# Pooled attention and a top-1 mixture of experts on one core: other buffers for the raw weights at the head, half tiles that fetch split weights into four sets of buffers, and a new order of issue

## The chip, the core and the metric

The kernel runs on one NeuronCore of a Trainium2 chip. The metric is the device time of one execution in microseconds. Inputs and outputs lie in the core's device memory (HBM). The engines are TensorE (PE), VectorE (DVE), ScalarE (ACT), GpSimd (POOL) and SyncE (SP, which here only starts transfers).

## What is computed

```python
# attention over pooled keys, B=4, 12288 queries each, C=128
kv_pool = kv.reshape(B, H // 4, 4, W // 4, 4, C).mean(axis=(2, 4))
k = v = kv_pool.reshape(B, -1, C) @ w_sr            # 768 keys per batch
s = (q @ k.transpose(0, 2, 1)) / np.sqrt(C)
a = np.exp(s - s.max(-1, keepdims=True)); a /= a.sum(-1, keepdims=True) + 1e-09
x = (a @ v).reshape(B * N, C)                        # 49152 rows of 128
# top-1 mixture of 8 experts, F=1024
logits = x @ w_gate
expert_idx = np.argmax(logits, axis=1)
out[mask_e] = gate_w[mask_e, None] * (np.maximum(x[mask_e] @ w1[e], 0.0) @ w2[e])
```

Here `gate_w` is the softmax probability of the chosen expert.

## The kernel before

All is float32. A product of two float32 matrices is made from three matmuls (`mm3`, lines 230 to 233): each operand is split into a high part (`high`, a rounding copy on ACT) and a low part (`low`, the source minus the high part, on DVE or POOL), and high times high, high times low and low times high add up in PSUM.

**The stages.** The 49152 rows are 96 stages of 512 rows, 24 to a batch. A stage of attention does the scores of four groups of 128 rows (`scores`), their maxima on DVE (`maxima`), the exponentials on ACT (`exps`), and then turns the probabilities: from stage 6 on DVE turns 32x32 blocks (`turn_p`), sixteen transfers move the blocks (`move_p`, tile pb to tile pt), ACT and POOL split them (`high_p` into tile pth, `low_p` in place in pt), and PE multiplies with the values (`values`). The first six stages turn them on PE instead (`turn_first`). Then `route` multiplies with the gate, picks each row's expert, counts places (`ranks`, `places`: the last part of `places`, called pos in the trace, is on POOL), and `put` scatters the rows with four GpSimd transfers into the buffer xs in HBM, sorted by expert. The row numbers that these need are reduced on DVE (tile dst, line 593). Before each stage's rows are filled POOL clears the tail of tile row (line 486), which waits for scatters under way.

**The experts.** From stage 2's end on, whenever 512 rows of an expert are there, `choose` (a chain of nine small DVE steps) picks an expert, and a tile of 512 rows goes through it: `read` loads the rows (tile xb) and their numbers (tokf), DVE turns them (xt, line 791), ACT and POOL split them (xh, xl), and eight blocks f of `first` (x times w1), `high_h` and `low_h` (tiles hh and hlow) and `second` (h times w2) follow. `copy_y`, `turn_y`, `rows_y` and `put` bring the result back to rows and scatter them into the output with GpSimd transfers (line 860) at the numbers in tile tok. There are 94 such full tiles. What is left at the end goes in half tiles of 256 rows (numbers 94 to 99 always, more only if rows are left); in a half tile the numbers are masked on DVE (lines 806 and 809, tile tok with 3 buffers).

**The weights.** At the head `split` (lines 148 to 173) loads each expert's raw w1 and w2 into tile raw (3 buffers, shared with the loads of keys), splits them on ACT and POOL into one of the two resident sets wts, and stores this set to ws in HBM (2 MB an expert). A full tile fetches its expert's set from ws (line 755) only if another expert than two tiles before was chosen. A half tile instead fetches the raw weights (`fetch_whole`, 1 MB) into pb and pt and splits them on the spot (`cut`, four pieces on ACT, and two each on POOL and DVE).

**The order.** `Plan` is a heap of steps, each with a time in units; 16 units are one stage. The table `AT` holds the offsets. Each engine gets its instructions in the order of these times on PE, ACT and DVE; the queues of POOL and SP follow the same plan through the scheduler. An engine works strictly in its own order: a step that waits holds up all behind it. A half tile comes every 8 units, and its expert is chosen shortly before it is fetched (line 894).

Of the kernel before, what the change touches and what calls it, by code (L numbers as in the profile page):

```python
# [21 lines left out]
P = 128  # L22
G = 4
# [9 lines left out]
    "turn_q": -0.15, "high_q": 3.34, "low_q": 5.01, "maxima": 1.13, "exps": 2.45, ("first_p", 0): 5.48,  # L33
    ("first_p", 1): 4.1, ("first_p", 2): 4.74, ("first_p", 3): 5.1, ("first_p", 4): 5.32,
    ("first_p", 5): 7.4, "first_high": 0.5, "first_low": 1.3, "first_values": 2.69, "turn_p": 2.65,
    "move_p": 17.32, ("high_p", 0): 28.78, ("high_p", 1): 25.01, ("high_p", 2): 29.02, "low_p": 0.45,
    ("values", 0): 37.6, ("values", 1): 38.01, ("values", 2): 39.41, ("values", 3): 39.91,
    ("values", 4): 41.61, ("values", 5): 42.21, "copy_x": 0.6, "turn_x": 1.76, "logits": 0.8, "row": 1.7,
    "gate_exp": 2.27, "gate": 2.29, "ranks": 1.12, "places": 2.13, "put_x": 3.83, "expert": 24.43,
    "fetch": -12.69, "read": -9.0, "weights": -5.6, ("cut", 0, 0): -7.93, ("cut", 1, 0): 3.67,  # L40
    ("cut", 0, 1): 1.14, ("cut", 1, 1): 3.1, "turn_m": -4.57, "high_m": 1.58, "low_m": 2.94, "first": 4.6,
    "high_h": 0.0, "low_h": 1.35, "second": 4.85, "copy_y": 0.52, "pads": 4.0, "split": -14.0, "splits": 11.0, "turn_y": 1.61, "rows_y": 4.66,
# [20 lines left out]
def tile_pooled_attention_top1_moe(ctx: ExitStack, tc, q, kv, w_sr, w_gate, w1, w2, out):  # L63
# [84 lines left out]
    def split(t, e):  # L148

        wt, own = wts[e % 2], {}  # L150

        def load():
            for n in range(2):
                own[n] = kp.tile([P, POOL // 2, POOL * C], F32, name="raw", bufs=3)
            nc.sync.dma_start(out=own[0].rearrange("p r c -> p (r c)"), in_=w1[e])
            nc.sync.dma_start(
                out=own[1].rearrange("p r (f d) -> p (r f) d", d=D),
                in_=w2[e].rearrange("(f p) d -> p f d", p=P),
            )

        def cut(n):
            wf = own[n].rearrange("p r c -> p (r c)")
            high(wt[:, 2 * n], wf)
            low(wt[:, 2 * n + 1], wf, wt[:, 2 * n], nc.gpsimd)
# [56 lines left out]
    def load_turned(name, rows, n):  # L221

        blocks = ap.tile([P, T], F32, name=name)
# [435 lines left out]
    def choose(j):  # L659
# [26 lines left out]
        if final:  # L686
# [7 lines left out]
            thr = rp.tile([P, 1], F32, name="thr" + tag, bufs=4)  # L694
# [3 lines left out]
        num = rp.tile([P, 3], I32, name="num" + tag)  # L698
# [42 lines left out]
    def weights(t, j):  # L741
# [17 lines left out]
        def fetch_whole():  # L759
            for n in range(2):  # L760
                own[n] = ap.tile([P, F], F32, name=("pb", "pt")[n])
            nc.sync.dma_start(out=own[0], in_=w1[bass.ds(own["ex"], 1)].rearrange("o p f -> p (o f)"))
            nc.sync.dma_start(
                out=own[1].rearrange("p (f d) -> p f d", d=D),
                in_=w2[bass.ds(own["ex"], 1)].rearrange("o (f p) d -> p (o f) d", p=P),
            )

        def cut(n, c):
            cs = slice(c * T, (c + 1) * T)
            high(wt[:, 2 * n, cs], own[n][:, cs])  # L770
            low(wt[:, 2 * n + 1, cs], own[n][:, cs], wt[:, 2 * n, cs], nc.vector if c else nc.gpsimd)

        at(t + AT["fetch"], where)
        if j < FULL:
            at(t + AT["weights"], fetch)
            return
        at(t + AT["fetch"], fetch_whole)
        for n in range(2):
            for c in range(F // T):
                at(t + AT["cut", n, c], cut, n, c)  # L780

    def experts(t, j):
        own = {}
        wt = wts[j % 2]
# [12 lines left out]
        def low_m():  # L797
# [3 lines left out]
            tok = own["tok"] = rp.tile([P, G], I32, name="tok", bufs=3)  # L801
            if own["thr"] is None:
                nc.gpsimd.tensor_copy(out=tok[:, gs], in_=own["tokf"][:, gs])
            else:
                old = rp.tile([P, G], F32, name="old")
# [5 lines left out]
        def first(f):  # L811
# [3 lines left out]
            hp = own["hp", f] = take()  # L815
            for k in range(per):
                fs = slice((f * per + k) * P, (f * per + k + 1) * P)
                mm3(hp[:, k * n : (k + 1) * n], wt[:, 0, fs], wt[:, 1, fs], own["xh"], own["xl"], True, True)
# [13 lines left out]
        def second(f):  # L832
            y = own["y"] = ps[:, BANK_Y, :n]
            for k in range(per):
# [3 lines left out]
                    y, wt[:, 2, fs], wt[:, 3, fs], own["hh", f][:, ns], own["hl", f][:, ns],  # L838
# [51 lines left out]

    def tile_j(j, u=None):
        t = 16 * (min(j, FULL) + AHEAD + 3) + 8 * max(j - FULL, 0) + AT["expert"]
# [3 lines left out]
        at(t + AT["read"], read, j)  # L896
        experts(t, j)
# [50 lines left out]
```

## Time and profile before

| what | value |
|---|---|
| median of 3 runs | 2346.57 us (2337.69 to 2347.06) |
| the profiled execution's own time | 2344.68 us |
| its span, first to last instruction | 2343.0 us |
| PE busy | 2179.0 us (93%) |
| POOL busy | 1832.5 us (78%) |
| DVE busy | 1777.1 us (76%) |
| ACT busy | 1494.3 us (64%) |
| mean granted TensorE clock | 0.986 |
| moved by the transfers | 324.59 MB |

A row of the timeline gives start and duration in us, engine, line, operation, what it writes and reads, and in brackets the engine's idle time before it and what ended that. A row of the waits gives in total how long one kind of instruction kept its engine idle for another, how often, and the longest. Lines are those of the kernel before.

### The profile page before, as it was taken

To read this page: it belongs to the slowest core of one execution; us is meant where nothing else is said; L and a number is where in the kernel's file an instruction comes from. 1 tells how busy PE (TensorE), PEld (TensorE's weight loads), DVE (VectorE), ACT (ScalarE), POOL (GpSimd) and SP (SyncE) were. 2 spreads that over 40 slices of the span, in tenths; PEclk is the share of its full clock that TensorE was granted. 3 is DMA by queue.
4 is the path that set the end of the run, shared out by engine and by line. 5 is a ranking of instruction groups with operands and counts; after the bars stand their busy time and mean duration, and the time that the engine had idled before them with its cause. 6 is when DMAs were issued, how large, how long until landed. Compare 5 with 4: busy or idle time off the path is not lost.

```text
span 2343.0 us, 41042 instructions
## 1 busy us (share of the span) xinstructions
PE 2179.0 (93%) x10630; PEld 1788.3 (76%) x10630; DVE 1777.1 (76%) x4368; ACT 1494.3 (64%) x3031; POOL 1832.5 (78%) x1957
## 2 busy tenths in 40 slices
PE   6778999999999999999999999999998999999986
PEld 6667877778777787778877777777786878788765
DVE  2566878987777778987786778998776777877564
ACT  2656666666666676666666666666665666666553
POOL 2656888878887888878887888878887888888863
PEclk9999999999999999999999999999999999999997
DMA  8866556655565556655556556665556555554341
GB/s 237 282 191 148 124 133 157 161 122 116 121 156 145 125 116 157 160 139 117 119 143 159 127 119 147 163 146 123 113 151 143 128 119 119 127 119 112 89 116 53
DMA packets 590357, 324.59 MB, mean 139 GB/s; under 512 B 497048, under 2 KB 515609, under 8 KB 588064
## 3 DMA queue, kind: packets, MB, share of 16 engines
q1 hardware_dynamic: 565408, 268.34, 51.0%
q0 software_dynamic: 24704, 53.53, 6.6%
q8 instruction: 87, 1.43, 0.3%
q14 instruction: 158, 1.29, 0.2%
HBM read 287.84 MB, written 72.88 MB: 154 GB/s over the span
## 4 chain that ended last, share of the span: by engine, by line
POOL 31%; PE 21%; DMA 13%; issue 13%; DVE 9%; SPq 8%; ACT 3%; POOLq 0%; DVEq 0%; ACTq 0%
POOL pt L219 18%; PE ps L231 7%; PE ps L232 6%; DMA xs<-row,dst 6%; PE ps L233 6%; POOL out_dram L860 5%; DMA xb<-xs 5%; POOL xs L595 4%; SPq L382 4%; SPq L226 3%; DVE hlow L826 3%; ACT prob L362 2%; POOL pos L586 1%; PE ps L500 1%; DVE pb L371 1%
## 5 line engine op out<-in xcount | busy, mean ns | idle before, releaser
L822 ACT ACTIVATE hh<-ps 128x512 fp32r<-128x512 f32 x776 | 465.3, 600 | 323.4 <-PE ps L233 309.8
L826 DVE SCALAR_TENSOR_TENSOR hlow<-ps,hh 128x512 fp32r<-128x512 f32 x776 | 529.1, 682 | 179.7 <-ACT hh L822 177.8
L219 POOL TENSOR_TENSOR pt<-pt,pth 128x1024 fp32r<-128x1024 f32 x270 | 640.4, 2413 | 2.8 <-ACT pth L216 1.8
L362 ACT ACTIVATE prob<-ps,nmax 128x768 f32<-128x768 f32 x384 | 346.2, 902 | 265.4 <-DVE nmax L354 265.2
L860 POOL DMA_INDIRECT out_dram<-yo,tok x388 | 384.8, 992 | 130.1 <-issue 79.9
L595 POOL DMA_INDIRECT xs<-row,dst x384 | 380.1, 990 | 116.1 <-issue 89.4
L371 DVE STREAM_TRANSPOSE pb<-prob 128x768 f32<-128x768 f32 x360 | 352.1, 978 | 88.5 <-ACT prob L362 78.6
L231 PE MATMUL ps<-xh,wt 128*128 128x512 f32 (+1 forms) x800 | 340.3, 425 | 75.2 <-DVE hlow L826 64.3
L354 DVE TENSOR_REDUCE nmax<-ps 128x1 f32<-128x768 f32 x384 | 364.7, 950 | 51.2 <-PE ps L233 49.9
L231 PE MATMUL ps<-hh,wt 128*128 128x512 f32 (+1 forms) x800 | 323.2, 404 | 0.0
L216 ACT CAST pth<-pt 128x1024 fp32r<-128x1024 f32 x270 | 273.4, 1047 | 69.6 <-DMA pt<-pb 55.2
L232 PE MATMUL ps<-hlow,wt 128*128 128x512 f32 (+1 forms) x800 | 314.1, 393 | 2.7 <-DVE hlow L826 2.7
L232 PE MATMUL ps<-xl,wt 128*128 128x512 f32 (+1 forms) x800 | 314.1, 393 | 1.5 <-POOL xl L219 1.5
L233 PE MATMUL ps<-xh,wt 128*128 128x512 f32 (+1 forms) x800 | 313.7, 392 | 0.0
L233 PE MATMUL ps<-hh,wt 128*128 128x512 f32 (+1 forms) x800 | 312.1, 390 | 0.0
L231 PE MATMUL ps<-kh,qh 128*128 128x384 f32 x768 | 269.7, 351 | 4.6 <-ACT qh L216 2.3
L232 PE MATMUL ps<-kl,qh 128*128 128x384 f32 x768 | 260.4, 339 | 0.0
L233 PE MATMUL ps<-kh,ql 128*128 128x384 f32 x768 | 259.6, 338 | 0.8 <-POOL ql L219 0.8
L231 PEld LDWEIGHTS ps<-xh,wt 128*128 128x128 f32 x800 | 153.4, 192 | 118.2 <-DVE hlow L826 95.1
L232 PE MATMUL ps<-pt,vh 128*128 128x512 f32 x540 | 213.8, 396 | 3.4 <-POOL pt L219 3.4
L231 PE MATMUL ps<-pth,vh 128*128 128x512 f32 x540 | 214.6, 397 | 0.0
L233 PE MATMUL ps<-pth,vl 128*128 128x512 f32 x540 | 213.8, 396 | 0.0
(133 smaller groups left out, 3824.6 us busy)
## 6 DMA issues: line engine op xcount, KB each, us to landing
wt<-ws SPq DMA_DIRECT2D x94, 2048.0 KB
pt<-pb SPq DMA_DIRECT2D x1440, 96.0 KB
raw<-in_kv_dram SPq DMA_DIRECT2D x96, 256.0 KB
qb<-in_q_dram SPq DMA_DIRECT2D x384, 64.0 KB
xb<-xs SPq DMA_DIRECT2D x376, 64.0 KB
ws<-wt SPq DMA_DIRECT2D x8, 2048.0 KB
raw<-in_moe_w_dram SPq DMA_DIRECT2D x16, 512.0 KB
out_dram<-yo,tok POOLq DMA_INDIRECT x388, 2.3
```

The lines of the kernel that those rows point to most:

```text
L216: nc.scalar.copy(out=dst, in_=src)
L219: eng.tensor_tensor(out=dst, in0=src, in1=h.bitcast(F32), op=ALU.subtract)
L231: nc.tensor.matmul(out=ps, lhsT=wh, rhs=xh, start=start, stop=False)
L232: nc.tensor.matmul(out=ps, lhsT=wh, rhs=xl, start=False, stop=False)
L233: nc.tensor.matmul(out=ps, lhsT=wl, rhs=xh, start=False, stop=stop)
L354: nc.vector.tensor_reduce(out=nmax, in_=own["s", g][:, :, :NH], op=ALU.max, axis=AX.XY, negate=True)
L362: nc.scalar.activation(out=prob.rearrange("p (h k) -> p h k", h=2), in_=own["s", g][:, :, :NH], func=AF.Exp, bias=own["nmax", g], scale=1. ...
L371: nc.vector.transpose(out=own["pb"][:, :, :, g, :].rearrange("p c b t -> p b c t"), in_=own["prob", g].rearrange("p (b c t) -> p b c t", c ...
L595: put = nc.gpsimd.indirect_dma_start(out=xs, out_offset=bass.IndirectOffsetOnAxis(ap=dst[:, g : g + 1].bitcast(U32), axis=0), in_=own["row ...
L822: nc.scalar.activation(out=hh, in_=own["hp", f], func=AF.Relu)
L826: nc.vector.scalar_tensor_tensor(out=hl, in0=own["hp", f], scalar=0.0, in1=own["hh", f].bitcast(F32), op0=ALU.max, op1=ALU.subtract,)
L860: put = nc.gpsimd.indirect_dma_start(out=out, out_offset=bass.IndirectOffsetOnAxis(ap=own["tok"][:, g : g + 1].bitcast(U32), axis=0), in_= ...
```

## The change

1. At the head the raw weights go to tile pth (4 buffers, which belong to the high parts of the probabilities and are first used in stage 6) instead of raw. The splits begin at -8 units instead of -14, at almost the same spacing (10.92 instead of 11); the cuts still come 10 and 11 units after the load, and the store to ws is placed 19 units after it instead of 14.
2. Half tiles fetch split weights from ws (2 MB, in two transfers of 1 MB for w1 and w2), with no condition and no `cut`. Tiles 94 and 95 take them into pb and pt, 96 and 97 into the two resident sets, 98 and 99 into pb and pt again. The fetch is placed 26 units before the tile, or where the tile four before it has ended, if that is later.
3. Half tiles read their rows into buffers of raw and prob instead of xb. The experts of tiles 94 to 99 are chosen right after those of the last full tiles, 4.6 units apart.
4. Buffers: tok, tokf and thr have 8 instead of 3, 3 and 4, num 4 instead of 2.
5. The table of offsets has new numbers. In a stage, `values` come up to 2 units earlier, the experts' rows are turned 2.5 units later (`turn_m`), the relu (`high_h`) comes 1.2 units later, `places` 0.8 earlier.

```diff
-    "turn_q": -0.15, "high_q": 3.34, "low_q": 5.01, "maxima": 1.13, "exps": 2.45, ("first_p", 0): 5.48,
+    "turn_q": 0.06, "high_q": 3.87, "low_q": 5.01, "maxima": 1.13, "exps": 2.45, ("first_p", 0): 6.3,
...
-                own[n] = kp.tile([P, POOL // 2, POOL * C], F32, name="raw", bufs=3)
+                own[n] = ap.tile([P, F], F32, name="pth", bufs=4)
...
-        at(t + 10, cut, 0)
-        at(t + 11, cut, 1)
-        at(t + 14, keep)
+        at(t + AT["split_cut"], cut, 0)
+        at(t + AT["split_cut"] + 1, cut, 1)
+        at(t + AT["split_keep"], keep)
...
-        own["xb"], gets = load_turned("xb", rows, size(j))
-        own["tokf"] = rp.tile([P, G], F32, name="tokf", bufs=3)
+        k = (j - FULL) % 6
+        own["xb"], gets = load_turned(*(("xb", rows, size(j)) if j < FULL else
+                                        ("raw", rows, size(j), kp) if k < 3 else ("prob", rows, size(j))))
+        own["tokf"] = rp.tile([P, G], F32, name="tokf", bufs=8)
...
-        def fetch_whole():
-            for n in range(2):
-                own[n] = ap.tile([P, F], F32, name=("pb", "pt")[n])
...
+        def fetch_end():
+            k = (j - FULL) % 4
+            if k < 2:
+                w1p = ap.tile([P, 2, F], F32, name="pb").bitcast(F32R)
+                w2p = ap.tile([P, 2, F], F32R, name="pt")
+            else:
+                w1p, w2p = wts[j % 2][:, :2], wts[j % 2][:, 2:]
+            own["wt"] = (w1p, w2p)
+            for n, w in enumerate(own["wt"]):
+                nc.sync.dma_start(
+                    out=w.bitcast(F32),
+                    in_=ws[bass.ds(own["ex"], 1)].rearrange("o p n f -> p (o n) f")[:, 2 * n : 2 * n + 2],
+                )
...
+        u = start(j - 4) + (size(j - 4) // 32 - 2) + AT["first"] + AT["second"] + 0.1
+        u = t + AT["fetch_end"] if j < FULL + 2 else max(t + AT["fetch_end"], u)
+        at(t + AT["fetch_end"], where)
+        at(u, fetch_end)
...
-            tok = own["tok"] = rp.tile([P, G], I32, name="tok", bufs=3)
+            tok = own["tok"] = rp.tile([P, G], I32, name="tok", bufs=8)
...
-        if ("tile", j) not in state:
-            select(t + AT["fetch"] - 6 if u is None else u, j)
+        if j < SURE:
+            state["chosen"] = state["chosen"] + 4.6 if u is None else u
+        if j != SURE:
+            select(state["chosen"] if j < SURE else t + AT["fetch_end"] - 6, j)
```

What the new numbers do to POOL's queue in a stage in the middle of the run, before (ql is the low part of the queries, xs the scatter of routed rows, row the clearing and numbering of the next rows, xl the low part of an expert tile's rows, out_dram the scatter of results, pt the low parts of the probabilities, pos the places):

```order
L219 TENSOR_TENSOR ql<-qt,qh 128x512
L803 CAST tok<-tokf 128x4
L595 DMA xs<-row,dst 397312x144 x4
L219 TENSOR_TENSOR xl<-xt,xh 128x512
L486 MEMSET row 128x4x15
L487 TENSOR_SCALAR row<-slot 128x4
L860 DMA out_dram<-yo,tok 49152x128 x4
L219 TENSOR_TENSOR pt<-pt,pth 128x4x256 x3
L586 TENSOR_TENSOR pos<-pos,oh 128x8 x3
```

and now:

```order
L218 TENSOR_TENSOR ql<-qt,qh 128x512
L594 DMA xs<-row,dst 397312x144 x4
L867 DMA out_dram<-yo,tok 49152x128 x4
L218 TENSOR_TENSOR xl<-xt,xh 128x512
L808 CAST tok<-tokf 128x4
L485 MEMSET row 128x4x15
L486 TENSOR_SCALAR row<-slot 128x4
L218 TENSOR_TENSOR pt<-pt,pth 128x4x256 x3
L585 TENSOR_TENSOR pos<-pos,oh 128x8 x3
```

The scatter of results moved ahead of xl and of the clearing of row, directly behind the scatter of routed rows. In the 18 stages that also load keys the clearing of row stands directly behind the scatter of routed rows in both kernels, and the scatter of results moved only ahead of xl.

SP's queue at the head, from the second load of weights on, before:

```order
L155 DMA raw<-in_moe_w_dram 128x1024
L141 DMA xs<-pad 512x1x144
L226 DMA qb<-in_q_dram 32x16x32 x4
L156 DMA raw<-in_moe_w_dram 128x8x128
L167 DMA ws<-wt_109 128x4096
L141 DMA xs<-pad 512x1x144 x6
L155 DMA raw<-in_moe_w_dram 128x1024
L156 DMA raw<-in_moe_w_dram 128x8x128
L226 DMA qb<-in_q_dram 32x16x32 x4
L167 DMA ws<-wt_110 128x4096
```

and now:

```order
L156 DMA pth<-in_moe_w_dram 128x1024
L157 DMA pth<-in_moe_w_dram 128x8x128
L225 DMA qb<-in_q_dram 32x16x32 x4
L141 DMA xs<-pad 512x1x144 x8
L225 DMA qb<-in_q_dram 32x16x32 x4
L166 DMA ws<-wt_109 128x4096
L156 DMA pth<-in_moe_w_dram 128x1024
L157 DMA pth<-in_moe_w_dram 128x8x128
L166 DMA ws<-wt_110 128x4096
L156 DMA pth<-in_moe_w_dram 128x1024
```

The eight fills of the pad rows moved ahead of the first store to ws, and no load of weights stands behind a fill any more.

SP's queue at the end, where the first half tiles are fetched (num holds the row, the expert and the condition of a chosen tile; the register instructions between are left out by name), now:

```order
L750 TENSOR_LOAD num
L771 DMA pb<-ws 128x2048
L771 DMA pt<-ws 128x2048
L225 DMA raw<-xs 32x8x32
L731 DMA tokf<-xs 128x2x1
L225 DMA xb<-xs 32x16x32
L731 DMA tokf<-xs 128x4x1
L757 DMA wt_110<-ws 128x4096
```

where before, tile by tile, stood:

```order
L748 TENSOR_LOAD num
L762 DMA pb<-in_moe_w_dram 128x1024
L763 DMA pt<-in_moe_w_dram 128x8x128
L226 DMA xb<-xs 32x8x32
L729 DMA tokf<-xs 128x2x1
```

The fetch and the rows of tile 94 moved ahead of the rows (xb) of the last full tile, 93.

More of the change, by code (lines that the diff above doesn't have):

```diff
@@ L32 @@
 AT = {
-    "turn_q": -0.15, "high_q": 3.34, "low_q": 5.01, "maxima": 1.13, "exps": 2.45, ("first_p", 0): 5.48,
[L34 to L42, printed above, removed]
+    "turn_q": 0.06, "high_q": 3.87, "low_q": 5.01, "maxima": 1.13, "exps": 2.45, ("first_p", 0): 6.3,
+    ("first_p", 1): 4.35, ("first_p", 2): 4.74, ("first_p", 3): 4.29, ("first_p", 4): 5.32,
+    ("first_p", 5): 7.4, "first_high": 0.5, "first_low": 1.3, "first_values": 2.69, "turn_p": 2.92,
+    "move_p": 17.32, ("high_p", 0): 28.78, ("high_p", 1): 25.01, ("high_p", 2): 29.02, "low_p": 0.53,
+    ("values", 0): 35.64, ("values", 1): 37.68, ("values", 2): 39.08, ("values", 3): 38.39,
+    ("values", 4): 41.28, ("values", 5): 41.88, "copy_x": 0.6, "turn_x": 2.27, "logits": 0.8, "row": 1.7,
+    "gate_exp": 2.27, "gate": 2.29, "ranks": 1.12, "places": 1.32, "put_x": 3.83, "expert": 24.43,
+    "fetch": -12.69, "read": -9.0, "weights": -5.6, "turn_m": -2.09, "high_m": 1.16, "low_m": 2.94, "first": 4.6,
+    "high_h": 1.2, "low_h": 1.35, "second": 4.85, "fetch_end": -26.0, "copy_y": 0.52, "pads": 4.0, "split": -8.0,
+    "splits": 10.92, "split_cut": 10.0, "split_keep": 19.0, "turn_y": 1.61, "rows_y": 4.66,
 }
@@ L219, in low, with load_turned @@
         eng.tensor_tensor(out=dst, in0=src, in1=h.bitcast(F32), op=ALU.subtract)
-    def load_turned(name, rows, n):
-        blocks = ap.tile([P, T], F32, name=name)
+    def load_turned(name, rows, n, pool=ap):
+        blocks = pool.tile([P, T], F32, name=name, bufs=3 if name in ("raw", "prob") else 2)
         bv = blocks[:, :n].rearrange("p (t c) -> p t c", c=SQ)
@@ L757, in fetch @@
             )
-        def fetch_whole():
-            for n in range(2):
-                own[n] = ap.tile([P, F], F32, name=("pb", "pt")[n])
[L762 to L773, printed above, removed]
+        def fetch_end():
[11 more added lines that the diff above has]
+                )
+        state["wt", j] = own
         if j < FULL:
+            own["wt"] = (wt[:, :2], wt[:, 2:])
+            at(t + AT["fetch"], where)
             at(t + AT["weights"], fetch)
             return
[L777 to L780, printed above, removed]
+        u = start(j - 4) + (size(j - 4) // 32 - 2) + AT["first"] + AT["second"] + 0.1
+        u = t + AT["fetch_end"] if j < FULL + 2 else max(t + AT["fetch_end"], u)
+        at(t + AT["fetch_end"], where)
+        at(u, fetch_end)
     def experts(t, j):
         own = {}
-        wt = wts[j % 2]
         n = size(j)
@@ L804, in low_m @@
             else:
-                old = rp.tile([P, G], F32, name="old")
+                old = table("old", G)
                 nc.vector.tensor_scalar(
@@ L837, in second @@
                 mm3(
[L838 removed]
+                    y, wt[:, 0, fs], wt[:, 1, fs], own["hh", f][:, ns], own["hl", f][:, ns],
                     fb == 0, fb == FB - 1,
@@ L889, in tiles, with start @@
             tile_j(i - AHEAD, u)
+    def start(j):
+        return 16 * (min(j, FULL) + AHEAD + 3) + 8 * max(j - FULL, 0) + AT["expert"]
     def tile_j(j, u=None):
-        t = 16 * (min(j, FULL) + AHEAD + 3) + 8 * max(j - FULL, 0) + AT["expert"]
-        if ("tile", j) not in state:
-            select(t + AT["fetch"] - 6 if u is None else u, j)
+        t = start(j)
+        if j < SURE:
+            state["chosen"] = state["chosen"] + 4.6 if u is None else u
+        if j != SURE:
+            select(state["chosen"] if j < SURE else t + AT["fetch_end"] - 6, j)
         weights(t, j)
-        at(t + AT["read"], read, j)
+        at(t + AT["read"] if j < FULL else t + AT["fetch_end"] + 0.1, read, j)
         experts(t, j)
```

16 lines of the change are left out of this document (8 added, 8 removed).

## Prediction

> **What bounds the kernel now.** I read the windows view first, over four pieces of the span that lie around what the change touches: the head with the splits, the 2000 us of full tiles, the last full tile, and the half tiles. A row gives the stretch, its length, then busy time and instructions of PE, PE's weight loads, DVE, ACT and POOL, then granted clock, DMA share and GB/s.
>
> ```profile
> 0.00:200.00 200.00, 144.23 (x807) 124.22 (x808) 101.44 (x258) 100.15 (x209) 95.17 (x119) 0.93 0.80 230
> 200.00:2200.00 2000.00, 1926.88 (x9251) 1571.99 (x9250) 1600.15 (x3872) 1328.95 (x2694) 1657.78 (x1756) 1.00 0.58 134
> 2200.00:2265.00 65.00, 59.31 (x267) 45.92 (x267) 37.42 (x130) 34.02 (x66) 45.12 (x51) 1.00 0.35 82
> 2265.00:2343.00 78.00, 48.61 (x311) 46.18 (x309) 38.04 (x110) 31.17 (x64) 34.44 (x33) 0.80 0.28 75
> ```
>
> PE is the bound wherever it is not idle, and its number of matmuls hardly changes. So the change can save no more than PE's idle time and what a lower clock costs. Idle are 200 - 144.23 = 55.8 us at the head, 2000 - 1926.88 = 73.1 us in the middle, 5.7 us in the third piece and 78 - 48.61 = 29.4 us in the half tiles, where the clock is 0.80 besides. Next came the waits view of the middle, to see what PE's idle time there is put down to (total us, times, longest).
>
> ```profile
> PE ps L231 <- DVE hlow L826: 44.3, 56, 2.5
> PE ps L849 <- DVE hlow L826: 13.4, 70, 0.5
> ```
>
> The first is the first matmul of a `first` block, which waits for the DVE step that frees its PSUM buffer. The timeline says why DVE is late, below.
>
> **The half tiles (parts 2, 3, 4).** First the waits view of DVE from 2264 on and then the timeline of PE and DVE. A timeline row is start, duration, engine, line, operation, and the idle time before it with its releaser.
>
> ```profile
> DVE tok L809 <- DMA out_dram<-yo,tok: 19.5, 4, 6.1
> 2264.85 0.28 PE L231 MATMUL ps<-xh,wt 128*128 128x256 f32 x1
> 2265.75 3.52 DVE L219 TENSOR_TENSOR wt<-pt,wt 128x512 fp32r<-128x512 f32 x1
> 2270.26 0.50 PE L232 MATMUL ps<-hlow,wt 128*128 128x512 f32 x1 [2.69 <-DVE hlow L826]
> 2271.24 0.42 PE L231 MATMUL ps<-xh,wt 128*128 128x256 f32 x1
> 2285.33 0.16 DVE L809 TENSOR_TENSOR tok<-old,tokf 128x2 int32<-128x2 f32 x1 [6.06 <-DMA out_dram<-yo,tok]
> 2287.19 0.58 PE L231 MATMUL ps<-xh,wt 128*128 128x256 f32 x1 [5.87 <-DVE hlow L826]
> 2287.57 0.42 PE L232 MATMUL ps<-xl,wt 128*128 128x256 f32 x1
> 2291.20 0.41 PE L231 MATMUL ps<-hh,wt 128*128 128x256 f32 x1
> 2292.08 0.28 PE L231 MATMUL ps<-xh,wt 128*128 128x256 f32 x1
> 2294.84 0.28 PE L233 MATMUL ps<-hh,wt 128*128 128x256 f32 x1
> 2332.77 0.37 ACT L844 COPY yt<-ps 128x256 f32<-128x256 f32 x1 [1.48 <-PE ps L233]
> ```
>
> Tile tok has 3 buffers. Its fourth user must wait until a scatter of results that reads the old numbers has landed; DVE stands for that four times, 19.5 us, and PE behind it, 5.87 us at 2287. After such a pause the matmuls are slow: from 2287.57 to 2291.20 seventeen of them take 3.63 us, 0.21 each, while the 23 steps from 2292.08 to 2294.84 take 0.12 each. Part 4 gives tok 8 buffers, and six half tiles follow the last full ones, so the wait goes, the pause goes, and with it the slow stretch, about 17 x 0.09 = 1.6 us a time. Part 2 takes all eight pieces of `cut` per half tile off ACT, POOL and DVE. One such piece on DVE, the 3.52 us at 2265.75, made PE wait 2.69 us.
>
> The new time of this piece: six half tiles of 48 matmuls each (eight blocks, two halves of the work, three matmuls) are 288 x 0.12 = 34.6 us. For the turns of the results and the lag of the first and last blocks I estimate 5 us. From the last copy at 2332.77 to the span's end at 2343.0 are 10.2 us, which no edit touches. That makes 50 us against 2343.0 - 2264.85 = 78.2 us now: **-28 us**. I take 1 us off for a late start and say **-27**.
>
> What is late next are the fetches. Six times 2 MB instead of six times 1 MB must come in. In the chain of waits at the head a fetch of the same kind has this row; the second row is the windows view where the present half tiles' weights come in.
>
> ```profile
> 180.13 9.18 DMA wt<-ws
> 2260.00:2270.00 10.00, 7.02 (x34) 5.55 (x34) 9.30 (x24) 5.53 (x12) 7.21 (x7) 1.00 0.71 184
> ```
>
> The first two fetches stand on SP ahead of the last full tile's rows, 26 units before their tiles, some 25 to 30 us, so at about 2240; six of 9.18 us are 55 us, so the last lands around 2295. With the time above the last half tile begins at 2264.85 + 5 x 5.8 = 2294, so the fetch just about does. At 184 GB/s, 2.1 MB take 11.4 us and six 68 us: the last lands at 2308, 14 us late for its first block, of which the wait for w2 lies further on; I price this case at 10 us, so -17. The Trainium skill (*DMA: Bandwidth & Descriptors*, Specifications) gives a core about 358 GB/s from HBM, by which a fetch would be an estimated 5.9 us, all six land before 2280 and never bind; the row of 9.18 us says less, and I go by the row. The last full tile's rows are queued behind such a fetch on SP, at most 9.18 us; the rows are asked for some 9 units, 12 us, ahead of their use, so this costs 0 to 3 us. Ends for the piece: -31 and -17.
>
> On the slow stretch the Trainium skill (*TensorE: Matmul & The Clock Gate*, Part 1) says that the clock halves after at least one idle window of about 3.4 us. The pause of 5.87 us agrees; behind the pause of only 2.69 us at 2270.26 the trace has slow matmuls too (0.42 at 2271.24, against 0.28), which speaks against the bound. By that rule new pauses of 2 to 3 us behind late fetches (R2) would cost no clock, by the row some 1.6 us each on top; with up to six of them that is inside the ends above.
>
> **The middle (part 5).** The timeline of a stage in which PE waits, in order of time:
>
> ```profile
> 711.60 0.15 POOL L486 MEMSET row<- 128x60 f32 x1 [3.22 <-DMA xs<-row,dst]
> 717.30 7.09 POOL L219 TENSOR_TENSOR pt<-pt,pth 128x1024 fp32r<-128x1024 f32 x3
> 724.36 0.75 POOL L586 TENSOR_TENSOR pos<-pos,oh 128x8 f32<-128x8 f32 x3
> 725.47 0.18 DVE L593 TENSOR_REDUCE dst<-pos 128x4 int32<-128x32 f32 x1 [3.80 <-POOL pos L587]
> 725.65 0.68 DVE L826 SCALAR_TENSOR_TENSOR hlow<-ps,hh 128x512 fp32r<-128x512 f32 x1
> 726.39 0.50 PE L231 MATMUL ps<-xh,wt 128*128 128x512 f32 x1 [2.16 <-DVE hlow L826]
> ```
>
> POOL stands 3.22 us at clearing row, since a scatter of routed rows has not landed. So its low parts end late, pos is late, DVE stands 3.80 us at dst, hlow behind it is late, and PE waits 2.16 us. Over the middle the same two waits read:
>
> ```profile
> POOL row L486 <- DMA xs<-row,dst: 92.5, 71, 5.6
> DVE dst L593 <- POOL pos L587: 88.1, 64, 4.2
> ```
>
> The order shows that now, in all but 18 stages, the scatter of results stands between the scatter of routed rows and the clearing of row. Its four pieces last from 1121.01 to 1125.89 in the rows of the next fence, 4.9 us, and with xl behind them POOL has 6 us of work there. 92.5 / 71 = 1.3 us a time, so most of this wait is covered. POOL then reaches its low parts earlier by up to what it waited, and a stage like the one above loses most of its 2.16 us. PE's `values` also stand one block further ahead, so the blocks that wait have about a block more of PE's work in front of them.
>
> How much of the 44.3 us goes? In the 18 stages with keys the clearing keeps its place and its wait stays, which leaves 50 to 53 of 71 stages helped, 0.7 to 0.75. Some of the wait is taken up again by POOL's own work, which is the same amount. I take 60%, **-26 us**. The ends are -44 (all of it) and +10 (the moved xl begins to cost, below). The 13.4 us at the turns of results (L849) are 0.19 us a time for the lag of hlow itself and stay.
>
> The price of the new order is on xl. A stage without that wait, POOL's queue from one pos to the next and PE's use of xl:
>
> ```profile
> 1111.02 0.75 POOL L586 TENSOR_TENSOR pos<-pos,oh 128x8 f32<-128x8 f32 x3
> 1118.54 1.32 POOL L219 TENSOR_TENSOR xl<-xt,xh 128x512 fp32r<-128x512 f32 x1
> 1121.01 1.06 POOL L860 DMA_INDIRECT out_dram<-yo,tok  x1 [0.46 <-ACT xt L430]
> 1123.41 0.40 PE L232 MATMUL ps<-xl,wt 128*128 128x512 f32 x1
> 1125.89 7.15 POOL L219 TENSOR_TENSOR pt<-pt,pth 128x1024 fp32r<-128x1024 f32 x3
> 1132.96 0.80 POOL L586 TENSOR_TENSOR pos<-pos,oh 128x8 f32<-128x8 f32 x3
> ```
>
> xl now ends at 1119.9, 3.5 us before PE reads it. Behind the scatter of results (1125.89 - 1121.01 = 4.9 us) it ends at 1124.8, 1.4 us after 1123.41, if POOL's queue started no earlier. But the places come 0.8 units earlier (16 units are the 21.94 us from 1111.02 to 1132.96, so 1.1 us), and the 0.46 and 0.35 us of small waits here go. So the two are about even: -1.4 + 1.1 + 0.5 = +0.2 us of slack. This is the step on which the forecast is least safe. I cost it at nothing, because a PE that waits here once moves its whole schedule later against POOL's and then has slack, unless POOL's own round is the longer one: 21.94 minus its waits of about 1 us is 20.9, below the period.
>
> Of what else moves, the queries' high parts and the relu (`high_h`) change only their place on ACT, which is idle a third of the middle (2000 - 1328.95), so nothing.
>
> **The head (part 1).** Rows of the timeline:
>
> ```profile
> 46.28 8.96 SPq L141 DMA_DIRECT2D xs<-pad  x6
> 61.37 1.04 ACT L216 CAST wt<-raw 128x1024 fp32r<-128x1024 f32 x1 [7.17 <-DMA raw<-in_moe_w_dram]
> 131.80 4.66 POOL L219 TENSOR_TENSOR wt<-raw,wt 128x1024 fp32r<-128x1024 f32 x2
> 138.46 1.09 PE L402 MATMUL ps<-ident,prob 128*128 128x128 f32 x4 [5.79 <-DVE num L700]
> ```
>
> ACT waited 7.17 us for raw weights queued behind other transfers, and PE behind its exponentials. The splits now begin 6 units later, so ACT does 4 to 6 us of other work first: I take -5. At 138.46 PE waited 5.79 us for a chain that begins with pos, which stood behind 4.66 us of the last split's low parts on POOL; in the new order pos stands ahead of them: -4 of 5.79. Together **-9 us**. The transfers of the head, 0.80 of the DMA engines' time by the first row, are the same in bytes, and the later stores no longer stand ahead of keys; if they now stand ahead of something that PE needs, as the six pads do in SP's queue for 8.96 us, it could cost 5. If all waits of this kind go it is -20. Ends: -20 and +5.
>
> **The sum.** -9 - 26 - 27 = -62 on the profiled execution. Its own time of 2344.68 becomes 2282.7; the median of the runs was 1.9 us above that execution, so **2284**, rounded down from 2284.6.
>
> **The rivals.**
> - R1, the middle gains nothing: POOL's wait goes, but DVE's dst was not what set PE's pace; its next wait is for ACT's hh. For it: the stages are within 3% of PE's busy time. Then -9 - 27 = -36, 2311. Against it: the chain at 711 to 726 is unbroken.
> - R2, the weights bind the half tiles at 184 GB/s: -17 in place of -27 and a middle at half, -13; -39, 2308.
> - R3, slower: PE waits for xl at each tile's first matmul. It decides from 36 / 94 = 0.4 us a tile on, since head and half tiles bring 36. With the 1.4 us of above less 0.5, 0.9 us in the 67 stages with the new order cost 60 us and the middle's gain goes: -36 + 60 = +24, 2371. Against it: the 1.1 us of the earlier places.
> - R4, the change doesn't do what it says in the half tiles: the copy to yo, with 2 buffers, waits for the same scatters as tok did, and DVE or ACT stands again. DVE stood up to 6.1 us for a landing, and half tiles are to be 5.8 us apart, so two buffers are near the edge. -17 for that piece, and 2294.
>
> **How the numbers follow.** Forecast 0.58, R1 0.20, R2 0.08, R3 0.06, R4 0.08. About 0.5%, 11.7 us, is what a measurement of this kernel can tell from no change. The low end of the range is the forecast with 8 of 20 us more of the head, 18 more of the middle and 4 of the half tiles: 2254 if all came at once, I say 2252. The high end takes in R1 with the half tiles at -17 and 0 to 2 us at the head lost: 2322. Outside lie R3 and the far ends, 2 in 10 at most. Faster holds the forecast, R2, R4 and nearly all of R1, and the milder edge of R3 is the same: faster 0.89, same 0.05, slower 0.06.
>
> **What would show it.** Right: in the half tiles no DVE wait at tok, clock near 1.0, and 50 us from the first of their matmuls to the end; in the middle, POOL's wait at row down from 92.5 to some 30 us (the 18 stages with keys), DVE's at dst under 45, PE's at L231 for hlow under 20; at the head no PE wait over 4 us behind POOL's low parts. Wrong: a new PE wait on POOL's xl in the waits view (R3), on a fetch of weights from ws after 2240 (R2), ACT waiting for out_dram at yo (R4), or PE's busy share of the middle still 96% with POOL's wait gone (R1).

## The result, and the profile after

The changed kernel takes **2307.65 us** (median of 4 runs, 2303.95 to 2310.3) against 2345.83 us for the kernel before in the same session: ratio 0.9845, 95% interval 0.9832 to 0.9858. The forecast was 2284 in a range of 2252 to 2322: the sign and the range held, the gain was 38 us where 62 were forecast. By the number alone R2 (2308) and R1 (2311) lie nearer than the forecast; which it was, only the waits can tell. The first four experiments (e1 to e4) ran on another chip than the later ones; there three kernels with the new table took some 300 us more than the same texts took elsewhere, so these three were run again. The gain of the changed kernel came back in its own second series (after_again).

I read the two profiles piece by piece, cut where the same work is done: at the dst step of stage 6, that of stage 92, and the first matmul of a half tile. The columns are those of the windows view. Before:

```profile
0.00:221.59 221.59, 165.65 (x911) 141.94 (x912) 116.70 (x292) 115.14 (x239) 109.69 (x132) 0.94 0.77 219
221.59:2174.66 1953.07, 1882.63 (x9042) 1536.01 (x9041) 1567.00 (x3790) 1299.41 (x2635) 1623.36 (x1721) 1.00 0.58 134
2174.66:2264.85 90.19, 82.01 (x372) 64.03 (x370) 55.16 (x180) 48.41 (x95) 65.00 (x73) 1.00 0.39 93
2264.85:2343.00 78.15, 48.76 (x311) 46.33 (x309) 38.19 (x110) 31.32 (x65) 34.46 (x34) 0.80 0.28 75
```

and the changed kernel:

```profile
0.00:208.04 208.04, 168.46 (x909) 143.77 (x910) 116.50 (x293) 113.86 (x238) 109.60 (x132) 0.92 0.82 232
208.04:2149.99 1941.95, 1871.15 (x9034) 1552.58 (x9033) 1581.09 (x3789) 1311.26 (x2633) 1615.54 (x1721) 0.99 0.58 135
2149.99:2254.65 104.66, 89.03 (x380) 69.75 (x380) 62.14 (x222) 48.54 (x93) 61.78 (x70) 0.93 0.48 126
2254.65:2308.60 53.95, 40.41 (x311) 38.74 (x309) 22.93 (x55) 20.97 (x44) 21.88 (x24) 0.91 0.43 141
```

The head won 13.6 us (forecast 9), the stages 6 to 92 won 11.1, the last full tiles **lost 14.5**, and the half tiles won 24.2 (forecast 27). Together 34.4 us of span (2343.0 to 2308.6). For the last full tiles the forecast had only 0 to 3 us for late rows. Taken with them, what it called the middle, 26 us of gain, came to 11.1 - 14.5, a loss of 3 us.

The two largest of PE's waits from stage 6 to stage 92 in the changed kernel, where the prediction shows those of before:

```profile
PE ps L230 <- DVE hlow L832: 25.1, 4, 6.4
PE ps L231 <- POOL xl L218: 24.4, 19, 2.8
```

The 44.3 us in 56 small waits are gone, and in their place stand four waits of over 6 us and 19 waits for xl. PE's idle time in this piece is as long as before, 70.8 us against 70.4. POOL's wait for the scatter and DVE's wait for pos behaved as forecast or better:

```profile
POOL row L485 <- DMA xs<-row,dst: 35.8, 18, 2.9
DVE dst L592 <- POOL pos L586: 0.9, 1, 0.9
```

92.5 us became 35.8, in just the 18 stages with keys, and 88.1 us became 0.9. So the chain that the prediction read was broken, and the time came back elsewhere. Where, is told by the step from dst to dst. Over 50 of the 60 stages that neither load keys nor change experts a stage took 22.13 us before and 21.42 now: 35 us won. Three stretches with keys (13 to 19, 36 to 43, 60 to 67) took 470.6 us together and now 513.2: 43 us lost. The third of them, rows of DVE in the kernel before and in the changed one:

```profile
1449.05 0.18 DVE L593 TENSOR_REDUCE dst<-pos 128x4 int32<-128x32 f32 x1 [1.21 <-POOL pos L587]
1612.86 0.17 DVE L593 TENSOR_REDUCE dst<-pos 128x4 int32<-128x32 f32 x1
```

```profile
1429.05 0.18 DVE L592 TENSOR_REDUCE dst<-pos 128x4 int32<-128x32 f32 x1
1611.42 0.18 DVE L592 TENSOR_REDUCE dst<-pos 128x4 int32<-128x32 f32 x1
```

163.8 us became 182.4. Inside such a stretch lies this, in order of time in the changed kernel (rows of POOL, DVE and PE):

```profile
893.37 1.32 POOL L218 TENSOR_TENSOR xl<-xt,xh 128x512 fp32r<-128x512 f32 x1
893.81 8.37 DVE L268 TENSOR_TENSOR pooled<-half 128x128 f32<-128x128 f32 x1
895.06 6.96 POOL L218 TENSOR_TENSOR pt<-pt,pth 128x1024 fp32r<-128x1024 f32 x3
902.11 0.68 DVE L832 SCALAR_TENSOR_TENSOR hlow<-ps,hh 128x512 fp32r<-128x512 f32 x1
902.84 0.80 PE L230 MATMUL ps<-xh,wt 128*128 128x512 f32 x1 [6.43 <-DVE hlow L832]
```

The DVE step that adds the two halves of a block of pooled keys (`join`) takes 8.37 us. It begins while POOL runs xl and ends when POOL's low parts end, at 902.0. In the kernel before the same step took a quarter of a microsecond:

```profile
938.44 0.25 DVE L269 TENSOR_TENSOR pooled<-half 128x128 f32<-128x128 f32 x1
938.63 0.97 POOL L860 DMA_INDIRECT out_dram<-yo,tok  x1 [0.31 <-issue]
940.89 7.09 POOL L219 TENSOR_TENSOR pt<-pt,pth 128x1024 fp32r<-128x1024 f32 x3
```

There it fell into the scatter of results, which stood between xl and the low parts; in the changed kernel xl and the low parts follow each other directly. Four of the 18 joins took 7.6 to 9.1 us in the changed kernel, and behind each PE stood for 6.1 to 6.4 us. At the last full tiles PE waits for xl, the longest for 6.25 us:

```profile
2222.95 0.79 PE L231 MATMUL ps<-xl,wt 128*128 128x512 f32 x1 [6.25 <-POOL xl L218]
```

**Theory.** (A) The new numbers win some 50 us in the stages without keys, those where experts change among them. The kernel loses it again by two things that POOL's new order brings: the low parts begin while DVE has its join, a step with two inputs in SBUF that does not get through while POOL computes, and xl stands behind the scatter of results, which makes PE wait in the stages with keys and at the last full tiles. (B) The rival: the stages with keys and the end are bound by DVE's and POOL's amount of work, the long rows are only where that shows, and whatever is taken away, another wait takes its place.

### The profile page after: what moved, and what is told of

Read it like the earlier page. It is cut to its first block, busy times and chain, and to the rows that moved or that the text cites. A ratio compares the mean times of both kernels' runs of the same rounds, so it can differ in the third digit from the quotient of the medians.

```text
span 2308.6 us, 40849 instructions
## 1 busy us (share of the span) xinstructions
PE 2169.1 (94%) x10630; PEld 1804.9 (78%) x10630; DVE 1782.7 (77%) x4356; ACT 1494.6 (65%) x3007; POOL 1808.8 (78%) x1945
## 5 line engine op out<-in xcount | busy, mean ns | idle before, releaser
L867 POOL DMA_INDIRECT out_dram<-yo,tok x388 | 379.4, 978 | 168.7 <-issue 88.8
L230 PE MATMUL ps<-xh,wt 128*128 128x512 f32 (+1 forms) x768 | 325.3, 424 | 41.1 <-DVE hlow L832 26.0
L230 PE MATMUL ps<-hh,wt 128*128 128x512 f32 (+1 forms) x768 | 321.1, 418 | 0.0
L231 PE MATMUL ps<-hlow,wt 128*128 128x512 f32 (+1 forms) x768 | 306.1, 399 | 0.0
L232 PE MATMUL ps<-xh,wt 128*128 128x512 f32 (+1 forms) x768 | 304.5, 397 | 0.0
L232 PE MATMUL ps<-hh,wt 128*128 128x512 f32 (+1 forms) x768 | 303.1, 395 | 0.0
L230 PE MATMUL ps<-pth,vh 128*128 128x512 f32 x540 | 215.6, 399 | 0.0
L231 PEld LDWEIGHTS ps<-xl,wt 128*128 128x128 f32 x768 | 147.4, 192 | 65.7 <-POOL xl L218 50.9
```

Of the source, the lines that this page charges most:

```text
L230: nc.tensor.matmul(out=ps, lhsT=wh, rhs=xh, start=start, stop=False)
L231: nc.tensor.matmul(out=ps, lhsT=wh, rhs=xl, start=False, stop=False)
L232: nc.tensor.matmul(out=ps, lhsT=wl, rhs=xh, start=False, stop=stop)
L867: put = nc.gpsimd.indirect_dma_start(out=out, out_offset=bass.IndirectOffsetOnAxis(ap=own["tok"][:, g : g + 1].bitcast(U32), axis=0), in_= ...
```

## The experiments

**e1_join and e7_join**, the same text: the join reads one tile by a reduction.

```diff
-            half = own["half", kb, h] = kp.tile([P, C], F32, name="half")
+            if h == 0:
+                own["half", kb] = kp.tile([P, 2, C], F32, name="half")
...
-            nc.vector.tensor_tensor(out=pooled, in0=own["half", kb, 0], in1=own["half", kb, 1], op=ALU.add)
+            nc.vector.reduce_sum(out=pooled, in_=own["half", kb].rearrange("p h c -> p c h"), axis=AX.X)
```

> The changed kernel, but the step that adds the two halves of the pooled keys (join, DVE) reads one tile with a reduction instead of two tiles with an addition. Theory A, a DVE step with two inputs in SBUF stands while POOL runs its low parts: the four joins that took 7.6 to 9.1 us take under 1 us, PE's four waits of 6.1 to 6.4 us for hlow go, and the kernel takes 2276 to 2284 us, 24 to 31 less than the changed kernel. Theory B, DVE is held at that place by something else, whatever the form of the step: the long steps stay, and the time stays within 5 us of 2307.7. Theory C, they go but the 18 stages with keys are bound by something else: the steps are short and the gain is under 10 us.

e1_join took 2587.42 us (2569.58 to 2602.75). Since e3_table and e4_xl_end, in the same session, were as slow, its time says nothing on the join; see e4. Its rows do: all 18 joins take 0.37 to 0.40 us, three of them beside POOL's low parts.

> The same text as the kernel e1_join (the join reads one tile by a reduction), since e1_join ran where every kernel with the new table lost some 280 us by pauses that the changed kernel's own runs do not have. Theory A, a DVE step with two inputs in SBUF stands while POOL runs its low parts: the four or five joins of 7.6 to 9.1 us take under 1 us, PE's waits of 6.1 to 6.4 us behind them go, 2270 to 2284 us, that is 24 to 37 less than the changed kernel. Theory B, DVE is held there whatever the form of the step: within 5 us of 2307.5. Theory C, the steps are short and the stages with keys are bound by something else: a gain under 10 us.

e7_join: **2280.89 us** (2279.52 to 2281.38), ratio to before 0.9755 (0.9738 to 0.9771), 26.5 us less than the changed kernel. All 18 joins take 0.38 to 0.41 us. Only three of them fell beside POOL's work, the one below wholly inside xl, so the test of the form rests on these three and the three of e1:

```profile
887.64 1.31 POOL L218 TENSOR_TENSOR xl<-xt,xh 128x512 fp32r<-128x512 f32 x1
888.14 0.38 DVE L269 TENSOR_REDUCE pooled<-half 128x128 f32<-128x256 f32 x1
```

PE's four long waits are gone, and the three stretches with keys take 479.3 us in place of 513.2. That is more than the 25.1 us of the four waits: the granted clock in the stretches is 1.00, where the changed kernel has 0.97, 0.98 and 0.95. Theory A; B falls for the joins. It is the form of the step, two inputs in SBUF against one, that decides.

**e2_old_table**: the changed kernel with the old numbers for the stages and tiles.

```diff
-    "turn_q": 0.06, "high_q": 3.87, "low_q": 5.01, "maxima": 1.13, "exps": 2.45, ("first_p", 0): 6.3,
+    "turn_q": -0.15, "high_q": 3.34, "low_q": 5.01, "maxima": 1.13, "exps": 2.45, ("first_p", 0): 5.48,
...
```

> The changed kernel with the old numbers in the table for the stages and tiles; the head's splits, the fetches of half tiles and the buffers stay changed. Theory A, the new numbers win about 54 us in the stages without keys and lose about as much in the stages with keys (43) and at the last full tiles (15): the time is within 10 us of the changed kernel, 2300 to 2316, with PE's waits at the first matmul for hlow back near 44 us and no wait for xl in the last tiles. Theory B, as the prediction had it, the new numbers bring 26 us in the middle and 4 at the head: 2332 to 2342.

2326.11 us (2325.09 to 2327.59), ratio 0.989 (0.9857 to 0.9923) to a kernel before of 2348.12: 22 us, between the two theories. The piece of the half tiles is as in the prediction:

```profile
2276.72:2325.90 49.18, 38.64 (x311) 37.46 (x309) 22.38 (x54) 20.55 (x44) 21.12 (x23) 0.95 0.45 156
```

49.2 us, where 50 were worked out. So the gain of the half tiles does not need the table; in front of them PE now waits 5.84 us once behind hlow, which takes part of it back. DVE stands 5.83 us there for the rows of the last full tile, the term that the prediction put at 0 to 3 us.

**e3_table and e9_table**, the same text: the kernel before with the new numbers alone.

```diff
-    "turn_q": -0.15, "high_q": 3.34, "low_q": 5.01, "maxima": 1.13, "exps": 2.45, ("first_p", 0): 5.48,
+    "turn_q": 0.06, "high_q": 3.87, "low_q": 5.01, "maxima": 1.13, "exps": 2.45, ("first_p", 0): 6.3,
...
```

> The kernel before with the new numbers of the table alone; splits, half tiles and buffers as before. Theory A, gains and losses cancel: within 10 us of the kernel before, 2336 to 2356, with the long joins and the waits for xl in the trace. Theory B, the prediction's term: 2312 to 2325.

e3_table: 2607.58 to 2660.29 us in four runs, with the same pauses as e4.

> The same text as the kernel e3_table: the kernel before with the new numbers of the table alone. Theory A, its gains in the stages without keys (54 us by the traces) and its losses in the stages with keys and at the last full tiles (43 and 15) cancel, with a few us from the head: 2328 to 2348 against 2342 before. Theory B, the prediction's term of 26 us in the middle and 4 at the head holds alone: 2308 to 2318.

e9_table: 2331.21 us (2324.54 to 2339.18), ratio 0.997 (0.9957 to 0.9983). Theory A: the table alone is worth 7 us. A stage without keys takes 21.38 us, the three stretches with keys 512.1, and five joins are long, four of them 8.3 to 9.1 us.

**e4_xl_end and e8_xl_end**, the same text: from tile 90 on the rows are turned at the old offsets.

```diff
-        u = t + AT["turn_m"]
+        early = j >= FULL - 4
+        u = t + (-4.57 if early else AT["turn_m"])
         at(u, turn_m)
-        at(u + AT["high_m"], high_m)
+        at(u + (1.58 if early else AT["high_m"]), high_m)
```

> The changed kernel, but from tile 90 on the rows are turned and split at the old offsets, so that xl stands ahead of the scatter of results on POOL again. Theory A, xl behind the scatter is what PE waits for at the last full tiles: the waits for xl after 2170 (17.6 us) go, and the kernel takes 2290 to 2298 us. Theory B, another wait takes their place, for rows, weights or the scatter: 2303 to 2310.

e4_xl_end took 2592.16 us (2584.38 to 2601.25), though up to tile 90 its order is that of the changed kernel. Its stages without keys last 23 to 28 us. The waits view of ACT from 200 to 2200 shows why, in a row that the changed kernel's trace doesn't have:

```profile
ACT hh L828 <- remote: 215.9, 48, 5.5
```

"remote" is what the profile prints when no recorded instruction fits the release. Once in most stages ACT stands for 3 to 5.5 us for a matmul that was long done by its record; DVE stands too. Neither theory speaks of this.

> The changed kernel once more, word for word. Three kernels with its table took 2587 to 2626 us, with pauses of 3 to 5 us on ACT and DVE once a stage that the profile puts down to nothing in the program; one of them differs from the changed kernel only from tile 90 on. Theory A, the pauses come from the state in which the chip ran, and the new table is sensitive to it: 2560 to 2630 us with the same pauses. Theory B, they come from the three edits: 2304 to 2311 us without them.

after_again, the changed kernel word for word: 2307.35 us (2301.32 to 2317.86) against 2339.41, ratio 0.9857 (0.9836 to 0.9878), without the pauses. That is theory B's number, but not its cause: e7, e8 and e9, the same texts as e1, e4 and e3, ran without the pauses too. So the three texts are cleared, and what the chip of e1 to e4 did stays open (last section). The trace of after_again has five long joins, of 8.3 to 9.1 us, three of them in other stages than in the first profile: a join is long or short by where POOL's work happens to fall.

> The same text as the kernel e4_xl_end (from tile 90 on xl stands ahead of the scatter of results on POOL again). Theory A: PE's waits for xl after 2170 (17.6 us in the changed kernel) go, 2290 to 2298 us. Theory B, another wait takes their place: 2303 to 2310 us.

e8_xl_end: **2287.33 us** (2283.08 to 2295.63), ratio 0.9786 (0.9758 to 0.9815), 20 us less than the changed kernel. The last full tiles and the half tiles:

```profile
2145.90:2240.39 94.49, 85.46 (x380) 66.58 (x379) 62.39 (x223) 48.51 (x93) 63.24 (x71) 0.98 0.51 139
2240.39:2288.10 47.71, 38.32 (x311) 37.38 (x309) 22.39 (x54) 20.93 (x44) 20.58 (x23) 0.93 0.45 159
```

104.66 and 53.95 us became 94.49 and 47.71, which is 16.4 of the 20 us. Theory A, 3 us below its range. What is left over the 90.19 of before is one pause: DVE stood for the rows of the last full tile, queued behind the first fetches.

```profile
2220.89 0.71 DVE L796 STREAM_TRANSPOSE xt<-xb 128x512 f32<-128x512 f32 x1 [4.53 <-DMA xb<-xs]
2222.31 0.50 PE L230 MATMUL ps<-xh,wt 128*128 128x512 f32 x1 [4.11 <-DVE hlow L832]
```

**e6_tok8**: the kernel before with 8 buffers for tok.

```diff
-            tok = own["tok"] = rp.tile([P, G], I32, name="tok", bufs=3)
+            tok = own["tok"] = rp.tile([P, G], I32, name="tok", bufs=8)
```

> The kernel before with 8 instead of 3 buffers for tile tok and nothing else. Theory A, the wait of the row numbers for scatters is what DVE, and PE behind it, stand for in the half tiles: DVE's 19.5 us at tok and PE's four pauses (5.87, 4.54, 3.11, 2.60 us) go with part of the slow clock, 12 to 24 us less than the kernel before. Theory B, the next thing that is late (the weights' cuts, the rows) takes their place: within 5 us of the kernel before.

2323.41 us (2321.39 to 2325.36), ratio 0.9932 (0.9915 to 0.9949): 16 us from one number. From the first matmul of a half tile to the end:

```profile
2261.51:2323.10 61.59, 43.74 (x311) 40.95 (x309) 42.13 (x110) 31.54 (x65) 34.84 (x34) 0.89 0.35 95
```

78.15 us became 61.6. Theory A. Two cuts on DVE of over 3.5 us remain, and take PE with them:

```profile
2262.20 3.75 DVE L219 TENSOR_TENSOR wt<-pt,wt 128x512 fp32r<-128x512 f32 x1
2280.23 3.58 DVE L219 TENSOR_TENSOR wt<-pt,wt 128x512 fp32r<-128x512 f32 x1 [0.40 <-ACT wt L216]
```

They too read two tiles in SBUF while POOL has its own cuts. Fetching split weights removes them; how much of the rest of the 24 to 30 us that brings, no run tested alone.

**e10_both**: e7_join, with xl ahead of the scatter from tile 90 on and in the stages with keys.

```diff
-        u = t + AT["turn_m"]
+        early = j >= FULL - 4 or j % SPB in (9, 10, 11, 12, 13, 14, 15, 16) and 9 <= j < 3 * SPB
+        u = t + (-4.57 if early else AT["turn_m"])
         at(u, turn_m)
-        at(u + AT["high_m"], high_m)
+        at(u + (1.58 if early else AT["high_m"]), high_m)
```

> The changed kernel with the join of e7_join, and xl ahead of the scatter of results from tile 90 on and in the stages with keys. Theory A, the two causes add up: 24 to 37 us from the joins, 10 to 15 from the last tiles, 10 to 20 from PE's waits for xl of 0.6 to 2.8 us in the stages with keys: 2240 to 2262 us. Theory B, with xl early the scatter of results ends later and POOL's low parts with it, so that the stages with keys win nothing more: 2262 to 2275.

**2245.62 us** (2244.1 to 2249.63), ratio to before 0.9609 (0.9593 to 0.9626): the fastest of the study, 62 us under the changed kernel. 26.5 of them are e7's, 20 e8's, and 13 are the three stretches with keys (479.3 to 466.0), where xl is in time again: from stage 6 to stage 92 PE waits 1.7 us for it, where e7 has 23.0. Theory A.

```profile
209.20:2101.80 1892.60, 1858.39 (x9036) 1543.65 (x9035) 1552.94 (x3790) 1310.64 (x2633) 1616.25 (x1721) 1.00 0.60 138
```

From stage 6 to stage 92 PE idles 34 us where it idled 71.

**e11_pool**: the kernel before with three of the new numbers, which alone give POOL its new order in the 66 stages.

```diff
-    ... "places": 2.13, ... "turn_m": -4.57, "high_m": 1.58, ...
+    ... "places": 1.32, ... "turn_m": -2.09, "high_m": 1.16, ...
```

> The kernel before with three of the new numbers, turn_m, high_m and places, which give POOL the changed order in the 66 stages without keys and leave PE's, DVE's and ACT's other steps where they were. From stage 75 to stage 91 a stage takes 22.13 us before and 21.33 in the changed kernel. Theory A, covering POOL's wait for the scatter is what shortens these stages: 21.2 to 21.6 us a stage. Theory B, the earlier values and the other numbers do it: 22.0 us or more here. Theory C, each does half: 21.6 to 21.9.

2389.06 us (2379.15 to 2394.54), ratio **1.0212** (1.0178 to 1.0246): slower than before. From stage 75 to 91 a stage takes 21.63 us, over the 50 stages 21.64: just inside theory C, some two thirds of the way to the changed kernel's 21.33. But nine joins take 7.4 to 8.8 us, and the three stretches with keys 550.0 us. The waits view of PE from 200 to 2200 (L838 is the turn of results):

```profile
PE ps L220 <- DVE hlow L815: 62.3, 27, 6.4
PE ps L838 <- DVE hlow L815: 12.8, 68, 0.5
```

**e12_rest**: the kernel before with all the other new numbers.

```diff
-    "turn_q": -0.15, "high_q": 3.34, ... ("values", 0): 37.6, ... ("values", 3): 39.91, ... "high_h": 0.0, ...
+    "turn_q": 0.06, "high_q": 3.87, ... ("values", 0): 35.64, ... ("values", 3): 38.39, ... "high_h": 1.2, ...
```

> The kernel before with all new numbers of the stages and tiles but those three, so that POOL keeps xl ahead of the scatter of results and, in half of the stages, the clearing of row too. Theory A: 21.9 to 22.2 us a stage, short joins in the stages with keys, and a time within 8 us of the kernel before. Theory B: 21.2 to 21.6 us a stage, 30 us or more less than the kernel before. Theory C: between.

2289.31 us (2281.61 to 2297.73), ratio **0.9803** (0.9776 to 0.983): 49 us less than before, which theory A had excluded. The stretches with keys take 455.7 us, and no join is long. In 75 to 91 a stage takes 21.34 us, theory B's figure, but POOL's rows in this trace speak for A after all: between two dst steps, from stage 8 to 91, POOL has the scatter of results ahead of the clearing of row 41 times and behind it 43 times. Of the 50 stages without keys or changes of expert the 31 of the first kind take 21.34 us each, the 19 of the second 21.88. So covering the wait for the scatter is worth 0.5 us a stage, with the other numbers (21.88 to 21.34) as without them (22.13 to 21.64 in e11), and the others are worth 0.25. The 19 all lie in stages 30 to 59; the kernel before shows no such difference there. The three theories priced all stages alike, though half of them have a new order here too. And in these the wait is covered with xl still ahead of the scatter. The waits at the turns of results, from 200 to 2200, belong to the other numbers:

```profile
PE ps L838 <- DVE hlow L815: 0.9, 4, 0.3
```

## Why the prediction was right or wrong

**The half tiles**: right in mechanism and size. 50 us were worked out, 53.95 came, 4.2 of them waits for xl; without these (e8) 47.7. No DVE wait at tok is left in the profile, no PE wait on a fetch after 2200 (R2) and no ACT wait for a scatter at yo (R4). The granted clock came to 0.91 (0.93 in e8), not near 1.0. e6 prices the tok wait at 16 us. The row of 3.52 us on DVE was read as a cost of `cut`. Rows of the kernel before show more:

```profile
2266.16 1.34 POOL L219 TENSOR_TENSOR wt<-pb,wt 128x512 fp32r<-128x512 f32 x1
2267.41 1.30 POOL L219 TENSOR_TENSOR wt<-pt,wt 128x512 fp32r<-128x512 f32 x1
2276.29 0.69 DVE L219 TENSOR_TENSOR wt<-pt,wt 128x512 fp32r<-128x512 f32 x1 [1.20 <-ACT wt L216]
```

DVE's eleven other cuts took 0.7 us each; the long one, from 2265.75 to 2269.27, stood beside POOL's two. That it was a wait for POOL, and so the key to the middle, I did not see.

**The head**: 13.6 for 9, inside its ends. PE's longest wait there is 5.5 us, for keys, as before; those of 8.29 and 5.79 us are gone. e2 and e9 take the two apart, with these waits of PE (e2, then e9):

```profile
115.10 1.09 PE L390 MATMUL ps<-ident,prob 128*128 128x128 f32 x4 [7.06 <-DVE num L688]
63.20 1.12 PE L391 MATMUL ps<-ident,prob 128*128 128x128 f32 x4 [7.61 <-ACT prob L351]
```

With the new buffers and splits but the old table (e2) the wait behind the exponentials is gone, the one behind num is not, and the dst step of stage 6 comes at 221.7 us, where it came at 221.6 before. With the table alone (e9) it is the other way round, and that step comes at 215.6. Only both together bring 208.0. So each part removes the wait that the prediction gave it, but the terms -5 and -4 don't simply add; which of the table's numbers does it was not tested.

**The middle** is the term that failed: -26 was taken, -11 came up to stage 92 and +14.5 behind it. That the time still lies in the range is owed to head and half tiles, 37.8 us where 36 were worked out, and to luck in the middle, where some 54 us won and 57 lost nearly cancel. Its gain was there, and larger than the term: 35 us in 50 stages, 12 more in the six where experts change, and 6 in the stages between. The reason given for it was right for two thirds of it (e11, e12): 0.5 of some 0.75 us a stage are the covered wait for the scatter; the rest comes with the other numbers. The 13.4 us at the turns of results, which the prediction let stay, go with them (12.8 in e11, 0.9 in e12, 0.5 in the changed kernel), and are about 0.2 us a stage; which of these numbers does it was not tested.

Two steps of the working failed. First, "I cost it at nothing", of xl behind the scatter: R3 was that mechanism, but I priced it over the 67 stages without keys, where it costs nothing, since PE's own work there fills 21.3 us. It bites where the working did not look: in the stages with keys (some 13 us, e10 against e7) and where the attention has ended and tiles follow each other faster (16 to 20 us, e8). Second, of the 18 stages with keys the prediction said only that they keep their wait. It asked what the earlier low parts would take away from POOL's waiting, and not what would now run beside them on DVE. The joins were never named; they cost 26.5 us (e7).

Of the signs of being wrong two came. PE waits for POOL's xl, which was R3's sign. And PE's busy share from stage 6 to stage 92 is 96% as before with POOL's wait gone, which was R1's, though not for R1's reason: in the 60 stages without keys or a change of experts PE's idle time fell from 27.7 to 4.4 us, and in the three stretches with keys it rose from 24.8 to 56.8. The time of those 60 stages fell by 41 us, more than their idle time held. So the premise that the change can save no more than PE's idle time and the cost of a lower clock was wrong as well: with the clock at 1.00 in both, PE's printed busy time fell by 18 us. Why was not tested.

**The slow clock**: the prediction weighed a rule against the row after a 2.69 us pause. The changed kernel speaks for the row again: a matmul that takes 0.40 us at the full clock takes 0.80 after the wait of 3.40 us for xl at 2241.52, and still 0.73 after one of 1.76 us at 2183.04; the granted clock from 2184 to 2186 is 0.50. The Trainium skill (*TensorE: Matmul & The Clock Gate*, Part 1) says that the clock halves after at least one idle window of about 3.4 us; the pause of 1.76 us, with one of 0.75 us shortly before it, does not agree.

```profile
2183.04 0.73 PE L231 MATMUL ps<-xl,wt 128*128 128x512 f32 x1 [1.76 <-POOL xl L218]
2241.52 0.80 PE L231 MATMUL ps<-xl,wt 128*128 128x512 f32 x1 [3.40 <-POOL xl L218]
```

## What to carry to other kernels

When an engine is made to start earlier, list what will now run beside it on the others, for each kind of stage and not for the common one alone: 18 stages with keys took back 43 of the 54 us that the others had won. A row that is long once and short eleven times, like DVE's cut, can be a wait without a name; find what ran beside it before calling it a cost. And price a moved step in every stretch where the pace differs, the last one above all: e12, without the new `turn_m`, `high_m` and `places`, beats the kernel with them (e9) by 42 us.

## What the runs showed of the hardware

A DVE addition with both inputs in SBUF that starts beside POOL's xl or low parts, or by its row up to 0.6 us before them (396.55 against 397.14 in the changed kernel), waits for POOL. 17 joins of the changed kernel, e9 and e11 took 7.4 to 9.1 us in place of 0.25. A reduction of the same bytes from one tile took 0.38 to 0.41 us beside the same POOL work (e7), and the addition took 0.25 to 0.29 us in the nine joins of the kernel before that began beside a piece of POOL's scatters. The Trainium skill (*SBUF — State Buffer*, Who interferes with whom) says that a DVE instruction with two SBUF inputs contends with a GpSimd instruction that reads SBUF, and that one with at most one, outside the modes that use both ports, doesn't; the runs agree. It also says that whoever issues first has the shared ports for the whole instruction; here the join that began at 893.81 stood through several, xl, the cast, the clearing of row and three low parts, until POOL had no next one. One join of e9 (357.20) got through after one low part, in 2.31 us, and one of the changed kernel that began late in xl (348.52) before the low parts, in 0.83.

The runs of e1, e3 and e4 show pauses of 3 to 7 us on ACT and DVE, once in most stages and only with the new table; on that chip e2, with the old table, had three of under 2 us, and the kernel before took 2348 us. In those traces many semaphore events are missing (of DVE's 4235 updates 3600 are recorded in e4's, 4196 in the changed kernel's); but e2's trace, without the pauses, has only 3150 of 4142. Whether the pauses come from the chip, from its state at the time or from how it was profiled was not settled, and which chip the changed kernel's first series ran on is not on record.
